# Key/value sums per head: four column-tiled matmuls of 33 columns in one PSUM bank, instead of one matmul of 129 columns over three banks

## The chip, the cores and the metric

One core of one Trainium2 chip. Times are device microseconds (us) of a whole execution, median of the runs named. The profile's span is about 1.7 us shorter than the time of the same execution (723.5 against 725.28 us for the kernel before). All runs here are with a granted TensorE clock of 0.999 to 1.0.

## The reference, cut to what matters

```python
# x: 1 x 2048 x 1024 bf16; 32 heads of 32; F = 3584
q, k, v = heads(layernorm(x) @ wqkv)
phi = lambda t: where(t > 0, t + 1, exp(t)) + 1e-6
kv  = einsum("bhsd,bhse->bhde", phi(k), v)      # 32 x 32 per head, summed over 2048 tokens
z   = einsum("bhsd->bhd", phi(k))
o   = (phi(q) @ kv) / (phi(q) @ z + 1e-6)       # per head
h   = x + o @ wo
out = h + (relu(h' @ W_gate) * (h' @ W_up)) @ W_down     # h' = layernorm(h)
```

The change touches the sums kv and z.

Some terms: a matmul multiplies a stationary operand, which a weight load brings in, by a moving operand. Its output goes to PSUM, here eight banks (0 to 7) of 128 partitions. In a row tile the stationary operand takes only some of the partitions that it is read from, in a column tile only some of the columns, and so the output only some of its partitions. A semaphore is a counter that one engine increments and another waits for.

## The kernel before

Tokens come in 16 tiles of 128. The projections k, v and q are computed in groups of seven products of 4 matmuls (128x128 by 128x512), called P1 to P7, for two token tiles at a time. ScalarE copies partial sums from PSUM bank to PSUM bank within a group, and TensorE adds to the copies. After the v group of a pair of token tiles, TensorE adds that pair to the key/value sums: eight head groups of four heads each, for each of two token tiles, so a block of 16 matmuls. There are eight such blocks.

A matmul multiplies all four heads of phi(k) by all four heads of v and a column of ones. Only the four 32x32 blocks on the diagonal, and the ones column, are wanted.

```python
KVB = [0, 1, 2]                  # three banks hold the sums
P1_POOL = [3, 4, 5, 6, 7]        # banks of the k and v groups

def kv_out(g, w=P + 1):          # GPB = 3 head groups per bank
    c0 = (g % GPB) * KZW
    return ps[:, KVB[g // GPB], c0:c0 + w]

def kvacc(st):                   # st: token tile
    sv = st % NV
    pa = pk_ap(st)               # phi(k) of this tile, 128 tokens x 1024
    for g in range(NG):          # 8 head groups
        ...
        mm(kv_out(g), pa[:, g * P:(g + 1) * P], vv[:, sv, g, 0:P + 1],   # 128x128 by 128x129
           first, st == NST - 1, ...)

def kvfin():                     # ten ScalarE copies pick out the diagonal blocks and the ones column
    ...
        for h in range(HPG + 1):
            ...
            copy(kvz[sl, g0:g0 + n, co]..., src[sl, :, :, cs])
    return steps
...
for h_ in (1, 3, 4, 7):          # spread over q groups two to four
    if kvc:
        hooks[h_] = kvc.pop(0)
```

`hooks[i]` is run after the i-th product of a group. The later attention numerators (`a2_num`) multiply phi(q) by these sums: 32 matmuls of 33 columns per token tile, in four row tiles of 32 partitions.

## Time and profile before

| what | number | where |
|---|---|---|
| time | 725.62 us (725.58 to 725.95, 4 runs) | runs |
| TensorE busy | 717.1 of 723.5 us | page, busy table |
| a block of key/value sums | 0.94 us, eight of them 7.5 us | timeline of TensorE |
| ten copies of the sums on ScalarE | 173 to 324 ns each | the tile's view |
| q groups beside the copies, and others | 6.28, 6.33, 6.51; 6.14 us | timeline of TensorE |

From the page, the busy table and the chain of work that ended last:

```profile
PE 717.1 (99%) x4521; PEld 384.6 (53%) x4521; DVE 587.2 (81%) x1024; ACT 361.0 (50%) x632; POOL 109.5 (15%) x177
PE 89%; DVE 6%; ACT 2%; issue 1%; SPq 1%; DMA 1%; POOL 0%; DVEq 0%; ACTq 0%
```

TensorE is busy nearly always, and the chain runs through it. The waits of TensorE (engine, who it waited for, total us, times, longest):

```profile
PE ps L767 <- POOL RXH L546: 1.4, 1, 1.4
PE ps L767 <- DVE RXH L1252: 0.7, 1, 0.7
PE ps L767 <- ACT ps L772: 0.2, 1, 0.2
```

So little is waited. Now one block in the timeline of TensorE. The columns are start in us, time until the last of the merged instructions ends, engine, line, operation, output and inputs, shape, and how many:

```profile
74.12 1.03 PE L767 MATMUL ps<-RW,RAB 128*128 128x512 f16 x4
74.99 1.10 PE L767 MATMUL ps<-RE 128*128 128x129 bf16 x16
75.93 1.02 PE L767 MATMUL ps<-RAB,RH 128*128 128x512 bf16 x4
76.79 1.03 PE L767 MATMUL ps<-RAB 128*128 128x512 bf16 x4
```

Read starts, not durations: ends are modelled and overlap the next instruction. From 74.99 to 75.93 us is 0.94 us for 16 matmuls, 58.7 ns each. A product of four matmuls of 512 columns takes 0.86 us by the same reading.

The numerators, in the same view (the second column of `32*128` is the stationary operand: 32 rows, 128 columns):

```profile
172.28 0.37 PE L767 MATMUL ps<-kvz,RAB 32*128 32x33 bf16 x32
172.58 3.63 PE L767 MATMUL ps<-RW,RE 128*128 128x512 bf16 x16
```

32 matmuls with 32 weight loads pass in 0.30 us, because four row tiles work at once.

Last, what the copies do. The timeline of ScalarE (ACT) and TensorE inside the fourth q group; PEld is the weight load, and brackets show idle time before and what ended it:

```profile
138.58 0.22 ACT L772 ACTIVATE kvz<-ps 32x64 bf16<-32x64 f32 x1
138.82 0.60 ACT L772 ACTIVATE RXH<-ps 128x512 f32<-128x512 f32 x1
...
139.31 0.59 ACT L772 ACTIVATE ps<-ps 128x512 f32<-128x512 f32 x1
...
139.95 0.55 PEld L767 LDWEIGHTS ps<-RWG,RH 128*128 128x128 f16 x4 [0.59 <-ACT ps L772]
139.96 1.04 PE L767 MATMUL ps<-RWG,RH 128*128 128x512 f16 x4
```

ScalarE does a small copy of the sums (kvz) first, then the two copies that belong to the group. The bank-to-bank copy (ps from ps) ends late, and TensorE starts its product at 139.96 instead of about 139.70, 0.86 us after the product before.

### The profile page before, as it was taken

Reading aid. Unit: us, or ns where it says so; the run is one execution under the profiler, and the core shown is the slowest. Engines: PE = TensorE matmul, PEld = TensorE weight load, DVE = VectorE, ACT = ScalarE, POOL = GpSimd, SP = SyncE. Lnnn points to the kernel's source line nnn. Section 1 sums busy time; section 2 is a strip of 40 time slices with the busy share of each in tenths; the row PEclk is TensorE's granted clock in tenths of the full one; section 3 lists DMA queues with packets and bytes.
Section 4 is the critical chain, followed back from the end, with each engine's and each line's share of the span. In section 5 each row is a group of like instructions: output and inputs, shape, how many; then the busy total and the mean of one; then the engine's idle time right before and its main releaser. Section 6 shows DMA issues by size and latency. Waiting matters only on the chain.

```text
span 723.5 us, 12104 instructions
## 1 busy us (share of the span) xinstructions
PE 717.1 (99%) x4521; PEld 384.6 (53%) x4521; DVE 587.2 (81%) x1024; ACT 361.0 (50%) x632; POOL 109.5 (15%) x177
## 2 busy tenths in 40 slices
PE   9999999999999999999999999999999999999998
PEld 4444444344444444444444568865555555547887
DVE  7878867799776889888988787787889877887984
ACT  4878666764841456687757111035455545423010
POOL 1411100000360103322321002310000000000331
PEclk9999999999999999999999999999999999999999
DMA  9652244023998897999999999994555572037996
GB/s 316 207 115 61 37 131 156 13 29 68 195 229 258 245 267 228 281 296 264 326 298 276 302 265 315 320 211 119 149 166 140 158 248 81 1 102 252 315 321 174
DMA packets 192986, 143.59 MB, mean 198 GB/s; under 512 B 51872, under 2 KB 170400, under 8 KB 192928
## 3 DMA queue, kind: packets, MB, share of 16 engines
q1 hardware_dynamic: 188224, 138.50, 66.6%
q0 software_dynamic: 4032, 3.67, 3.6%
q8 instruction: 35, 0.57, 0.3%
q10 hardware_dynamic: 672, 0.66, 0.3%
q14 instruction: 23, 0.19, 0.1%
HBM read 98.76 MB, written 32.51 MB: 181 GB/s over the span
## 4 chain that ended last, share of the span: by engine, by line
PE 89%; DVE 6%; ACT 2%; issue 1%; SPq 1%; DMA 1%; POOL 0%; DVEq 0%; ACTq 0%
PE ps L767 89%; SPq L565 1%; DVE RAB L853 1%; DMA RE<-in_A_x_dram 1%; DVE RE L1228 1%; DVE RX L850 1%; ACT RX L846 1%; DVE RX L1069 1%; ACT RXH L805 1%; DVE RW L963 0%; DVE RWG L988 0%; ACT ps L772 0%; DVE RE L853 0%; DVE rden L1226 0%; DVE RE L1661 0%
## 5 line engine op out<-in xcount | busy, mean ns | idle before, releaser
L772 ACT ACTIVATE ps<-ps 128x512 f32<-128x512 f32 (+1 forms) x192 | 108.8, 567 | 218.0 <-PE ps L767 210.8
L767 PE MATMUL ps<-RC,RO 128*128 128x512 f16 x616 | 143.0, 369 | 0.0
L767 PE MATMUL ps<-RH,RWG 128*128 128x512 bf16 x448 | 108.1, 379 | 0.0
L767 PEld LDWEIGHTS ps<-RC,RO 128*128 128x128 f16 x616 | 60.3, 98 | 63.5
L767 PE MATMUL ps<-RC,RWG 128*128 128x512 f16 x320 | 76.8, 380 | 0.1
L767 PEld LDWEIGHTS ps<-RH,RWG 128*128 128x128 bf16 x448 | 43.8, 98 | 46.9
L767 PE MATMUL ps<-RH,RO 128*128 128x512 bf16 (+1 forms) x256 | 61.2, 379 | 0.0
L1470 DVE TENSOR_TENSOR RAB<-ps,RAB 128x512 bf16<-128x512 f32 x56 | 37.3, 686 | 29.4 <-PE ps L767 29.3
L767 PE MATMUL ps<-RW,RE 128*128 128x512 bf16 x256 | 57.6, 380 | 0.7 <-DVE RXH L1252 0.7
L1670 POOL DMA_DIRECT2D out_dram<-RX x20 | 17.9, 1256 | 263.3 <-DVE RX L1661 221.0
L767 PE MATMUL ps<-RAB 128*128 128x512 bf16 (+2 forms) x270 | 57.1, 351 | 0.1
L767 PE MATMUL ps<-RW,RAB 128*128 128x256 f16 (+3 forms) x362 | 52.9, 301 | 0.0
L767 PEld LDWEIGHTS ps<-RC,RWG 128*128 128x128 bf16 (+1 forms) x320 | 30.0, 98 | 40.0 <-ACT ps L772 6.0
L772 ACT ACTIVATE RE<-ps 128x512 f32<-128x512 f32 (+1 forms) x64 | 31.5, 503 | 37.8 <-PE ps L767 37.8
L767 PEld LDWEIGHTS ps<-RW,RAB 128*128 128x128 f16 (+1 forms) x362 | 35.4, 98 | 14.4 <-DVE RX L1661 0.2
L1354 DVE TENSOR_TENSOR RO<-RWG 128x1024 f16<-128x1024 bf16 x54 | 37.0, 684 | 6.4 <-DMA RWG<-in_B_W_up_dram 4.7
L1661 DVE TENSOR_TENSOR RE<-ps,RE 128x512 f32<-128x512 f32 x44 | 30.2, 687 | 14.3 <-PE ps L767 13.8
L772 ACT ACTIVATE RAB<-ps 128x512 bf16<-128x512 f32 x56 | 33.3, 594 | 16.6 <-PE ps L767 16.3
L767 PEld LDWEIGHTS ps<-RH,RO 128*128 128x128 f16 (+1 forms) x256 | 24.4, 98 | 30.0 <-ACT RX L772 1.6
L1456 DVE TENSOR_TENSOR RAB<-ps,RE 128x512 bf16<-128x512 f32 x56 | 37.1, 685 | 2.8 <-PE ps L767 1.9
L767 PEld LDWEIGHTS ps<-RW,RE 128*128 128x128 bf16 x256 | 24.0, 98 | 28.7 <-DVE RXH L1252 1.2
L1465 ACT ACTIVATE RAB<-RAB 128x1024 bf16<-128x1024 bf16 x28 | 29.5, 1055 | 19.4 <-DVE RAB L1456 18.9
(163 smaller groups left out, 1168.7 us busy)
## 6 DMA issues: line engine op xcount, KB each, us to landing
RWG<-in_B_W_gate_dram SPq DMA_DIRECT2D x28, 512.0 KB, 6.8
RWG<-in_B_W_up_dram SPq DMA_DIRECT2D x28, 512.0 KB, 5.5
RW<-l_scr SPq DMA_DIRECT2D x20, 448.0 KB, 5.8
RW<-in_B_W_down_dram SPq DMA_DIRECT2D x14, 512.0 KB, 5.7
t_scr<-RW SPq DMA_DIRECT2D x14, 512.0 KB, 5.0
l_scr<-RX SPq DMA_DIRECT2D x7, 1024.0 KB, 5.9
RE<-l_scr SPq DMA_DIRECT2D x15, 448.0 KB, 4.5
RE<-in_A_x_dram SPq DMA_DIRECT2D x23, 256.0 KB, 3.3
```

The costliest lines, as they stand in the source:

```text
L565: return PL.add(eng, lambda e: e.dma_start(dst_ap, src_ap), reads=reads, writes=writes, slot=slot, name=name)
L767: lambda e: e.matmul(out_ap, lhsT, rhs, start=start, stop=stop, skip_group_check=skip),
L772: PL.add("act", lambda e: e.activation(out=dst, in_=src, func=func), reads=reads, writes=writes, name=name)
L805: PL.add("act", lambda e: e.activation(out=junk[:, c0:c1], in_=src[:, c0:c1], func=func, scale=scale, accum_out=sv[:, col:col + 1]), reads ...
L846: PL.add("act", lambda e: e.activation(out=Et[:, k, :], in_=src, func=ACTF.Exp), reads=[src_buf], writes=[B_E[k]], name=name + "_exp")
L850: PL.add("dve", lambda e: e.tensor_scalar(out=Et[:, k, :], in0=Et[:, k, :], scalar1=1.0, scalar2=1e-6, op0=ALU.min, op1=ALU.add), reads=[] ...
L1354: PL.add(eng, lambda e: e.tensor_tensor(out=tb(j, u), in0=f0(u), in1=f1(u), op=ALU.subtract), reads=[B_w[i + x] for x in r] + ([B_T[k + x] ...
L1456: PL.add("dve", lambda e: e.tensor_tensor(out=d, in0=src, in1=ftmp[:, u, :], op=ALU.add), reads=[bsrc, B_s5[u]], writes=[db], name=name)
L1465: PL.add("act", lambda e: e.activation(out=d, in_=d, func=ACTF.Relu), reads=[], writes=db, name=name)
L1470: PL.add("dve", lambda e: e.tensor_tensor(out=d, in0=bank(b), in1=d, op=ALU.mult), reads=[B_bank[b]], writes=[db], name=name)
L1661: PL.add(eng, lambda e: e.tensor_tensor(out=dst, in0=in0, in1=in1, op=op), reads=reads, writes=writes, name=name)
L1670: PL.add("pool", lambda e: e.dma_start(dst, src, accum_op=ALU.add), reads=[bsrc], writes=[B_hscr[st]], slot=sl, name="acc_%d_%d" % (st, dh))
```

## The change

Its intent: compute only the diagonal blocks. Each head's 32 columns of phi(k) become one column tile of TensorE, with output in that head's 32 partitions, and the moving operand is that head's 32 columns of v and a column of ones. That needs v stored in runs of 33 instead of 130 columns per head group. The sums fit one bank, one copy evacuates them, and two banks go to the k and v groups.

```diff
+    HW = Dh + 1                      # 33
+    VW = HPG * HW
@@
-        KVB = [0, 1, 2]
-        P1_POOL = [3, 4, 5, 6, 7]
+        KVB = 0
+        P1_POOL = [1, 2, 3, 4, 5, 6, 7]
@@ def kvacc(st):
-                mm(kv_out(g), pa[:, g * P:(g + 1) * P], vv[:, sv, g, 0:P + 1],
-                   first, st == NST - 1, [B_pk[pk_slot(st)][half], B_v[sv][half], B_vones], B_bank[kb],
-                   "kvacc_%d_%d" % (st, g), skip=True)
+                for h in range(HPG):
+                    c0 = g * P + h * Dh
+                    mm(ps[h * Dh:(h + 1) * Dh, KVB, g * HW:(g + 1) * HW], pa[:, c0:c0 + Dh],
+                       vh[:, (st % NV) * H + g * HPG + h, :], False, st == NST - 1,
+                       [B_pk[pk_slot(st)][half], B_v[st % NV][half], B_vones], B_bank[KVB],
+                       "kvacc_%d_%d" % (st, g), skip=True)
@@ def kvfin():           (the ten copies, cut)
+            touch_bank(KVB)
+            ident_act(kvz[:, :, 0:HW], ps[:, KVB, 0:NG * HW].rearrange("p (g w) -> p g w", w=HW), [B_bank[KVB]],
+                      [B_kvz], "kvc")
@@
-        pe_dummies(12, P1_POOL)
+        pe_dummies(12, P1_POOL + [KVB])      # also zeroes the bank of the sums
@@
-                if r == 0 and ct == 1:
-                    kvc = kvfin()
-                if r == 0 and ct >= 1:
-                    for h_ in (1, 3, 4, 7):
-                        if kvc:
-                            hooks[h_] = kvc.pop(0)
+                if r == 0 and ct == 1:
+                    hooks[1] = kvfin
```

The v copies and the column of ones are adapted to the new layout (cut).

More of the change, by code (lines that the diff above doesn't have):

```diff
@@ L171, in bass_sequential_preLN__linear_attn_block__glu_gated_reglu__prompt_kernel @@
     NKV = 2 * ND2
-    VW = P + 2
-    KZW = P + HPG
-    GPB = 3
+    HW = Dh + 1
+    VW = HPG * HW
     GPN = NW // P
@@ L265, in bass_sequential_preLN__linear_attn_block__glu_gated_reglu__prompt_kernel @@
         o0 += NPK * D
-        vv = RE[:, o0:o0 + NV * NG * VW].rearrange("p (a g w) -> p a g w", a=NV, g=NG)
+        vh = RE[:, o0:o0 + NV * NG * VW].rearrange("p (n w) -> p n w", w=HW)
         def pk_slot(st):
@@ L412, in bass_sequential_preLN__linear_attn_block__glu_gated_reglu__prompt_kernel @@
         B_E = bufs("E_", NPH)
-        B_kvz = bufs("kvz_", 2 * (HPG + 1))
+        B_kvz = _Buf("kvz")
         B_pqT = [[bufs("pqT%d_%d_" % (r, t), NG) for t in range(2)] for r in range(2)]
@@ L555, in bass_sequential_preLN__linear_attn_block__glu_gated_reglu__prompt_kernel @@
         )
-        PL.add("pool", lambda e: e.memset(vv[:, :, :, P:VW], 1.0), writes=[B_vones], name="vones")
+        PL.add("pool", lambda e: e.memset(vh[:, :, Dh:HW], 1.0), writes=[B_vones], name="vones")
         PL.add("pool", lambda e: e.memset(neghalf[:], -0.5), writes=[B_neghalf], name="neghalf")
@@ L860, in phi @@
                 f_()
-        KVB = [0, 1, 2]
-        P1_POOL = [3, 4, 5, 6, 7]
-        def kv_out(g, w=P + 1):
-            c0 = (g % GPB) * KZW
-            return ps[:, KVB[g // GPB], c0:c0 + w]
+        KVB = 0
+        P1_POOL = [1, 2, 3, 4, 5, 6, 7]
         def run(ops, n):
@@ L945, in v_out @@
         def v_out(st, j):
-            return vv[:, st % NV, j * GPN:(j + 1) * GPN, 0:P]
+            n0 = (st % NV) * H + j * GPN * HPG
+            return vh[:, n0:n0 + GPN * HPG, 0:Dh]
         def gw(ap):
-            return ap.rearrange("p (g w) -> p g w", w=P)
+            return ap.rearrange("p (n w) -> p n w", w=Dh)
         def v_copy(b, st, j):
@@ L1164, in q_group @@
                    add_phi(*dst(1, 1), "q_%d_%d" % (r, ct)), "q%d%d" % (r, ct), hooks)
-        kv_started = [False] * 8
         def kvacc(st):
-            sv = st % NV
             pa = pk_ap(st)
@@ L1172, in kvacc @@
                 half = (g * P) // NW
-                kb = KVB[g // GPB]
-                first = not kv_started[kb]
-                kv_started[kb] = True
-                mm(kv_out(g), pa[:, g * P:(g + 1) * P], vv[:, sv, g, 0:P + 1],
-                   first, st == NST - 1, [B_pk[pk_slot(st)][half], B_v[sv][half], B_vones], B_bank[kb],
-                   "kvacc_%d_%d" % (st, g), skip=True)
-        def kvfin():
-            for b_ in KVB:
-                touch_bank(b_)
-            rb = [B_bank[b_] for b_ in KVB]
-            steps = []
-            def copy(out, in_):
-                b_ = B_kvz[len(steps)]
-                steps.append(lambda: ident_act(out, in_, rb, [b_], "kvc"))
-            for b0, nb, ng, g0 in ((0, 2, GPB, 0), (2, 1, NG - 2 * GPB, 2 * GPB)):
-                src = ps[:, b0:b0 + nb, 0:ng * KZW].rearrange("p b (g w) -> p b g w", w=KZW)
-                n = nb * ng
-                for h in range(HPG + 1):
-                    sl = slice(h * Dh, (h + 1) * Dh) if h < HPG else slice(0, P)
-                    cs = sl if h < HPG else slice(P, P + 1)
-                    co = slice(0, Dh) if h < HPG else slice(Dh, Dh + 1)
-                    copy(kvz[sl, g0:g0 + n, co].rearrange("p (b g) w -> p b g w", b=nb), src[sl, :, :, cs])
-            return steps
-        A_POOL = [[3, 4, 5, 6, 7], [4, 5, 6, 7]]
+                for h in range(HPG):
[4 more added lines that the diff above has]
+                       "kvacc_%d_%d" % (st, g), skip=True)
+        def kvfin():
+            touch_bank(KVB)
+            ident_act(kvz[:, :, 0:HW], ps[:, KVB, 0:NG * HW].rearrange("p (g w) -> p g w", w=HW), [B_bank[KVB]],
+                      [B_kvz], "kvc")
+        A_POOL = [P1_POOL[2:], [4, 5, 6, 7]]
         NB = [0, 1, 2, 3]
@@ L1213, in a2_num @@
                     mm(ps[:, NB[h], g * NUW:g * NUW + Dh + 1], pqT[sl, r, t, g, i * P:(i + 1) * P],
-                       kvz[sl, g, 0:Dh + 1], True, True, [B_pqT[r][t][g]] + B_kvz, B_bank[NB[h]],
+                       kvz[sl, g, 0:Dh + 1], True, True, [B_pqT[r][t][g], B_kvz], B_bank[NB[h]],
                        "num_%d_%d" % (st, g), skip=True)
```

## The prediction

> What bounds the kernel now. TensorE. The page's busy table gives PE 717.1 of 723.5 us (99%), the chain that ended last is 89% PE, and the view of waits shows 2.3 us of PE waits, 0.2 us of them between 20 and 170 us. A microsecond of TensorE stream removed there should come off the end.
>
> Where the change works. The timeline of TensorE shows eight blocks of sixteen 128x129 matmuls (two token tiles times eight head groups) between 35 and 124 us. From the start of a block to the start of the next matmul is 0.94 us (35.24 to 36.18, 48.67 to 49.61), 58.7 ns per matmul. All eight: 7.5 us, 1.0% of the span. That is nearly the whole prize.
>
> After: each block is 64 weight loads of 32 columns and 64 matmuls of 33, in sixteen sets of four column tiles. The kernel has a similar stream already: the attention numerators, 32 matmuls of 33 columns in four row tiles. In the trace's single start times each set of four takes 25 ns there (172.316, .341, .366, .391), and from the last start to the next ordinary matmul is 0.10 us. The Trainium skill, "TensorEngine Tiling (Array Packing)", Key Properties, says that different tiles can load weights and multiply in parallel and that changing the tiling mode drains TensorE; the trace agrees for row tiles (25 ns for four; about 0.1 us on leaving). The same page, Restrictions and Gotchas, says that column tiling excludes Fast Weight Load; no trace here has a column tile, so this is my largest doubt.
> My estimate for a block, if column tiles run like row tiles: 16 x 25 ns = 0.40, plus 0.10 to leave, up to 0.1 to enter and for waits in the stream: 0.60 us. Saved: 0.34 x 8 = 2.7 us.
>
> The copies of the sums on ScalarE: ten (173 to 324 ns, by the tile's view) become one of 128x264, estimated 0.38 us from the shapes measured (32x64 210 ns, 32x192 318 ns). Between 123 and 143 us they delay the bank-to-bank copies that TensorE waits for: the q groups without them take 6.14 us, the three with them 6.28, 6.33 and 6.51, 0.70 us lost. The one copy costs about 0.1 of that again. Saved: 0.6 us.
>
> Moved, expected to cost nothing: the values are written in runs of 32 instead of 128 (VectorE's similar op with runs of 32 takes 1225 ns per 1024 elements, against 690 per 512); two PSUM banks are freed, but TensorE hardly waits for a bank; 384 more weight-load and matmul pairs are fetched and dispatched.
>
> Sum: 725.6 - 2.7 - 0.6 = 722.3; with some weight on slower column tiles I say 722.8 us, 80% range 721.2 to 727.0. Faster by over 2%: 1%; within 2%: 96%; slower by over 2%: 3%.
>
> What would show it: in the timeline the eight blocks as 64 matmuls of 128x33, about 0.6 us to the next matmul, 25 ns per set of four; all q groups near 6.14 us; VectorE and ScalarE times per instruction unchanged; everything after 148 us about 3 us earlier.
>
> What would make it wrong: weight loads of column tiles going one after another (at 25 ns each a block takes about 1.7 us: 731 in all); dispatch of 128 instructions not keeping up; 66-byte steps that misalign the odd heads and slow the moving reads or value writes; the earlier work turned into waits for the weight DMAs after 169 us (DMA engines are 93 to 98% busy from 169 to 460 us).

## The result, and the profile after

723.75 us (723.53 to 723.92, 4 runs) against 725.62: 1.87 us less. The ratio of the fast runs is 0.9973, 95% interval 0.9956 to 0.999. A ratio here is the mean time of one kernel's fast runs over that of the other's of the same rounds, so not quite the ratio of the medians. The result of the kernel is correct.

The page's lines:

```profile
PE 714.2 (99%) x4905; PEld 380.4 (53%) x4905; DVE 587.5 (81%) x1024; ACT 359.2 (50%) x623; POOL 108.4 (15%) x177
PE 90%; DVE 6%; issue 1%; ACT 1%; POOL 1%; DMA 0%; ACTq 0%; DVEq 0%
```

384 more matmuls, 9 fewer ScalarE instructions, the same bound. The waits of TensorE (line numbers are shifted by the change):

```profile
PE ps L766 <- POOL RXH L545: 1.4, 1, 1.4
PE ps L905 <- DVE RXH L834: 1.1, 1, 1.1
PE ps L766 <- DVE RXH L1229: 0.7, 1, 0.7
PE ps L766 <- ACT ps L771: 0.5, 1, 0.5
PE ps L766 <- DVE RWG L984: 0.4, 1, 0.4
```

Three waits are new or longer: 1.1, 0.5 and 0.4 us. All lie before 40 us. The same block as above:

```profile
74.22 1.03 PE L766 MATMUL ps<-RW,RAB 128*128 128x512 f16 x4
75.18 0.70 PE L766 MATMUL ps<-RE 128*32 128x33 bf16 x64
75.81 1.04 PE L766 MATMUL ps<-RAB,RH 128*128 128x512 bf16 x4
76.69 1.03 PE L766 MATMUL ps<-RAB 128*128 128x512 bf16 x4
```

Two things are to be seen. The block itself takes 75.18 to 75.81, 0.64 us. And the product ahead of it lasts 74.22 to 75.18, 0.96 us instead of 0.86: entering the column-tiled stream costs 0.09 us. So a block costs 0.73 us, not 0.94. All eight blocks are alike to 2 ns.

Why 0.64? These are the times from one set of four matmuls to the next in this block, in ns, from the start times of single matmuls (the last figure includes 110 ns from the last matmul to the next ordinary one):

```
set       1   2   3   4   5   6   7   8 |  9  10  11  12  13  14  15   16
after    38  25  25  26  25  27  25  26 | 33  37  33  56  36  34  33  159
```

The first eight sets go at 25 ns, like the row tiles of the numerators. From the ninth on a set takes 33 to 37 ns, and two sets have about 22 ns more; the matmul that comes late is each time one that increments a semaphore.

The copies of the sums, in the tile's view, are one (min, median and max ns; first and last start), where before it had ten:

```profile
L771 ACT ACTIVATE kvz<-ps x1: 387/387/387, 124.8 to 124.8; 128x264 bf16<-128x264 f32 x1
```

Q groups two to four now take 6.20, 6.15 and 6.13 us. The value writes in runs of 32 cost nothing: medians of 687 to 694 ns on VectorE and 595 ns on ScalarE, against 684 to 691 and 592.

To see where a gain or a loss arises, I compare starts of the same VectorE instruction, whose order is the same in all kernels here. The lead is how much earlier it starts than in the profile of before:

| at (us in before) | 12.9 | 46.6 | 61.3 | 89.8 | 107.5 | 122.3 | 142.3 | 189 | 338 | 720 |
|---|---|---|---|---|---|---|---|---|---|---|
| lead of after | -0.32 | -0.32 | -0.18 | +0.04 | +0.41 | +0.57 | +1.41 | +1.43 | +1.43 | +1.44 |

It starts 0.32 us behind, because the first load of x ended later in this execution (VectorE's first instruction starts at 3.59 us, in before at 3.27). Until 46.6 us the lag stays 0.32 to the hundredth: the first block's saving does not show. From there the lead grows, and what is gained by 142 us stays to the end.

### The profile page after: what moved, and what is told of

The parts are those of the page before. It is cut to its first block, busy times and chain, and to the rows that moved or that the text cites. A ratio compares the mean times of both kernels' runs of the same rounds, so it can differ in the third digit from the quotient of the medians.

```text
span 722.1 us, 12877 instructions
## 1 busy us (share of the span) xinstructions
PE 714.2 (99%) x4905; PEld 380.4 (53%) x4905; DVE 587.5 (81%) x1024; ACT 359.2 (50%) x623; POOL 108.4 (15%) x177
## 4 chain that ended last, share of the span: by engine, by line
PE 90%; DVE 6%; issue 1%; ACT 1%; POOL 1%; DMA 0%; ACTq 0%; DVEq 0%
PE ps L766 90%; DVE RAB L852 1%; DVE RE L1205 1%; DVE st L780 1%; DVE RX L849 1%; POOL rstd L790 0%; DVE RW L959 0%; DMA RE<-in_A_x_dram 0%; DVE RC L959 0%; DVE RX L1065 0%; ACT RX L845 0%; ACT RXH L804 0%; DVE RXH L834 0%; DVE rden L1203 0%; ACT ps L771 0%
## 5 line engine op out<-in xcount | busy, mean ns | idle before, releaser
L766 PEld LDWEIGHTS ps<-RAB 128*128 128x128 bf16 (+1 forms) x270 | 26.0, 98 | 24.4 <-ACT RAB L908 1.0
```

Of the source, the lines that this page charges most:

```text
L766: lambda e: e.matmul(out_ap, lhsT, rhs, start=start, stop=stop, skip_group_check=skip),
```

## The experiments

Theory. (1) A block costs 0.73 us because the first 64 instructions (32 pairs of weight load and matmul) stand ready when it starts, and from then on the issue of instructions limits: about 8.3 ns per pair, more for one that increments a semaphore. (2) The first block's saving is lost since VectorE sets the pace up to about 40 us. (3) The copies gave back what they cost. Rivals are named with each run. All were timed in five rounds, in three series; the time of before in them was 725.99, 725.75 and 725.92 us. Each has one profile. In the profiles of most of these runs the record of the first matmul after six of the eight blocks is missing (4849 of 4905 matmuls recorded), so where I give a block's time I take it from the two that have it.

### rep_after: the changed kernel again

> The changed kernel again, unaltered: 723.75 +- 0.3 us. It gives a second profile, to see how much of the start varies by itself: the first load of x ended 0.32 us later in the profile of after than in that of before, and VectorE stayed exactly 0.32 us late until 42 us. If that is chance of the load, the offset is another one here (0.0 to 0.4 us); if the change causes it, it is 0.32 again. The blocks must again take 0.64 us from their first matmul to the next ordinary one.

723.95 us (723.79, 723.80, 723.95, 724.05, 725.00). Blocks 0.638 us. VectorE's first instruction starts at 3.49 us, in the other twelve profiles of changed kernels between 3.33 and 3.59. So it varies from execution to execution; the profile of before, at 3.27, had the earliest of all. The start is not the whole lag, though: in nine of the thirteen VectorE loses another 0.04 to 0.28 us at about 27 us. In the profile of rep2_after (below) the lag goes from 0.06 to 0.32 us there: ScalarE waits 1.00 us for a load of x at 21.44 us, TensorE then waits for ScalarE, and at 28.20 us VectorE does. Whether this second part is chance or comes with the change, the one profile of before does not tell. One execution in five was 1 us slower, but its span, 722.0 us, is that of the others: what it lost lies outside the span, so it is not the late transposes of below.

### g_outer: another order of the same 64 pairs

```diff
         def kvaccs(p):
-            kvacc(2 * p)
-            kvacc(2 * p + 1)
+            for g in range(NG):
+                kvacc(2 * p, [g])
+                kvacc(2 * p + 1, [g])
```

> In each block the head group is the outer loop and the token tile the inner one (same 64 pairs, another order). Theory (the first 64 instructions stand ready when the block starts, from then on issue limits): pairs 1 to about 33 again at 25 ns per set of four, the rest at about 33 ns, block 0.64 us, time 723.7 +- 0.3. Rival A (adding to columns that the set just before also added to is slow): every second set slow from the start. Rival B (the second token tile's addresses are slow): every second set slow from the start, the block as long as now.

723.95 us (one execution of 725.01, again with a span of 722.0); blocks 0.639 us. The sets of a block:

```
set       1   2   3   4   5   6   7   8 |  9  10  11  12  13  14  15   16
g_outer  40  25  25  25  25  25  25  29 | 33  37  33  34  33  33  56  161
```

The change of pace is at the same place although other data stand there: rivals A and B fall. The longer set has moved from 12 to 15, to where this order has its increments; the increments that fall within the first eight sets cost nothing.

### split: two bursts of 32 pairs

```diff
                 def v6(p=p, nq=nq):
-                    kvaccs(p)
+                    kvacc(2 * p)
...
-                v_group(p + 2, {2: v2, 3: v3, 5: v5, 6: v6})
+                v_group(p + 2, {2: v2, 3: v3, 5: v5, 6: v6, 7: lambda p=p: kvacc(2 * p + 1)})
```

(and likewise for the last two blocks)

> The two token tiles of a block are put one product of 4 matmuls apart, so two bursts of 32 pairs. Theory (queue of 64 instructions, then issue-bound): all sets of both bursts at 25 ns; each burst 0.09 to enter + 0.21 + 0.10 to leave = 0.40, two 0.80 instead of 0.73 us, so 0.5 us slower than after in all (724.2). Rivals (the second token tile is slow for its addresses or for adding to written columns): second burst at 33 ns per set, 0.90 us for both, 1.2 us slower (724.9).

724.47 us, 0.52 more than rep_after beside it. The timeline of TensorE:

```profile
75.47 0.38 PE L766 MATMUL ps<-RE 128*32 128x33 bf16 x32
76.01 0.81 PE L766 MATMUL ps<-RAB,RH 128*128 128x512 bf16 x3 [0.16 <-issue]
76.75 0.38 PE L766 MATMUL ps<-RE 128*32 128x33 bf16 x32
77.06 0.60 PE L766 MATMUL ps<-RAB 128*128 128x512 bf16 x2
```

(In the second line the first of four matmuls is not recorded, hence "x3" and a wait that was none.) Both bursts run all their sets at 25 ns, the second token tile too. A burst takes 0.31 us and 0.09 to enter, two 0.81 us instead of 0.73. The theory's number was 0.80. This run settles the main point of (1): the slow half is a matter of how many pairs follow one another, not of which. That it is the issue of instructions that limits there is inferred from the count of 64 and the even pace; no record shows it. It shows as well that the fast pace alone does not pay, as each burst pays for entering and leaving.

### one_inc: one increment per block instead of four

The last matmul of a block is noted as the reader of everything that the block read, so the earlier ones need not increment.

```diff
+        def last_reads(st):
+            return [b for s_ in ([st - 1, st] if st % 2 else []) for b in B_pk[pk_slot(s_)] + B_v[s_ % NV]]
...
-                       [B_pk[pk_slot(st)][half], B_v[st % NV][half], B_vones], B_bank[KVB],
+                       [...] + (last_reads(st) if g == NG - 1 and h == HPG - 1 else []), B_bank[KVB],
```

> A block's readers are noted at its last matmul, so that one matmul of 64 increments the semaphore instead of four. Theory (in the issue-bound half an increment costs about 22 ns more of issue): the pause of 31 ns in the middle of the second half goes, the block takes 0.61 instead of 0.64 us, 0.2 us faster in all (723.5). Rival (the pauses come from the waits or the place in the stream): the pause stays, time as after.

723.48 us, 0.47 less than rep_after. Blocks 0.597 us; sets 9 to 15 all take 31 to 38 ns, and the 56 is gone. The lead at 142 us is 1.75 instead of 1.42 us. The pause came from the increment.

### two_tiles: two column tiles of 64

```diff
-                for h in range(HPG):
+                for h in range(0, HPG, 2):
...
-                    mm(ps[h * Dh:(h + 1) * Dh, KVB, g * HW:(g + 1) * HW], pa[:, c0:c0 + Dh],
-                       vh[:, (st % NV) * H + g * HPG + h, :], ...
+                    mm(ps[h * Dh:(h + 2) * Dh, KVB[g // 4], (g % 4) * 2 * HW:(g % 4 + 1) * 2 * HW], pa[:, c0:c0 + 2 * Dh],
+                       vh[:, n0:n0 + 2, :], ...
```

(KVB is [0, 1], six banks for the groups, four copies of 32x264 at products 1 and 3 of the second q group and 1 of the next two)

> Two column tiles of 64 instead of four of 32: 32 pairs a block, 66 moving columns, output in two banks, four copies of 32x264. Theory (the first 64 instructions stand ready, a set lasts as long as its columns stream: 66 columns about 30 ns): 16 sets of 30 ns, block 0.59 us from first matmul to the next ordinary one instead of 0.64, 0.3 us gained in the blocks, 0.2 to 0.3 us lost to the copies: time as after within 0.3 us. Rival (a weight load of 64 columns[...] is slower than the stream): sets of 50 ns or more, block 0.9 us, 1.5 us slower than after.

724.56 us. The sets of two take 29 to 36 ns, 32 on average, the block 0.63 us. By the products' pace (216 ns for 512 columns) I estimate 28 ns for 66 columns, so this is near the pace of the stream; the rival (50 ns or more) falls, and weight loads of 64 columns are nearly hidden. But the gain over 0.64 is little, and the copies cost far more than I expected: between 122 and 142 us its lead goes from 1.12 to 1.06 us, where that of after grows by 0.84. The expected time was missed by 0.3 us for the copies.

### ten_copies: the old copies in the changed kernel

```diff
+            for g0, n in ((0, 6), (6, 2)):
+                for h in range(HPG):
+                    copy(slice(h * Dh, (h + 1) * Dh), g0, n, 0, Dh)
+                copy(slice(0, P), g0, n, Dh, HW)
...
+                    for h_ in (1, 3, 4, 7):      # as before
```

> The changed kernel, but the sums are copied out in ten pieces of the shapes of before, at the same places in the q groups. Theory: q groups two to four take 6.28, 6.33 and 6.5 us again instead of 6.15, the kernel is 0.6 to 0.7 us slower than after (724.6). Rival (the q groups got faster by the freed banks or by an earlier VectorE): no more than 0.2 us slower.

724.70 us. No run of after stood in this series (ten_copies, skip1, skip4 and five_banks); in the other two it took 723.95 and 723.92. The lead at 142 us is 0.81 instead of 1.41 us: the copies are worth 0.60 us (0.66, if the lead is counted from 46.6 us on), nearly all of the 0.70 us that the q groups lost before. (3) holds.

### skip1 and skip4: one block left out

Their outputs are wrong, which doesn't matter for the times.

```diff
         def kvaccs(p):
+            if p == 0:          # skip4: p == 3
+                return
             kvacc(2 * p)
```

> Wrong result on purpose: the changed kernel without the first block of the key/value sums (0.73 us of TensorE at 35 us). Theory (up to about 40 us VectorE, which starts with the first load of x and never idles, decides when TensorE may go on): TensorE waits the 0.73 us away at the first product after it that needs VectorE or ScalarE, time within 0.15 us of after. Rival (TensorE binds throughout): 0.73 us faster.

> Wrong result on purpose: the changed kernel without the fourth block (0.73 us of TensorE at 75 us). Theory (TensorE binds from about 47 us on): 0.55 to 0.73 us faster than after, a little lost to gaps as TensorE moves ahead of ScalarE and VectorE. Rival (VectorE binds there as well): under 0.3 us faster.

By the time both missed: 724.72 and 724.54 us, each slower than after in the other two series. The profile takes this apart:

| lead (us) at | 46.6 | 142.3 | 189 | 338 | 720 |
|---|---|---|---|---|---|
| after | -0.32 | 1.41 | 1.43 | 1.43 | 1.44 |
| skip1 | -0.32 | 1.39 | 1.41 | 0.03 | 0.05 |
| skip4 | -0.19 | 2.21 | 2.24 | 0.68 | 0.68 |
| five_banks (below) | -0.30 | 1.70 | 1.72 | 0.81 | 0.82 |

Up to 189 us both theories hold. Without the whole first block, 0.73 us of TensorE, skip1 leads as after does: that block is off the critical path. Without the fourth, skip4 leads by 0.80 us more (0.67, counted from 46.6 us on). One product of TensorE starts at 39.39 us with the first block and without it, in after and then in skip1 (which had also waited 0.22 us more at 33.88 us, just before the place of the block):

```profile
39.39 1.04 PE L766 MATMUL ps<-RC,RWG 128*128 128x512 f16 x4 [0.53 <-ACT ps L771]
```

```profile
39.39 1.04 PE L766 MATMUL ps<-RC,RWG 128*128 128x512 f16 x4 [0.96 <-ACT ps L771]
```

That the first block is off the critical path, as (2) has it, is shown. That VectorE sets the pace there is so only in part: ScalarE is busy without a pause before this product, since a wait for VectorE that ended at 36.95 us; but VectorE does idle before that (0.5 to 1.0 us at 12, 20 and 22 us), and in nine profiles it loses time at about 27 us, as said above. But then, between 189 and 338 us, skip1 loses 1.4 and skip4 1.6 us. The waits in the timeline of TensorE, skip1 and then skip4:

```profile
199.68 3.61 PE L766 MATMUL ps<-RW,RE 128*128 128x512 bf16 x16 [0.62 <-DMA RE<-RE]
...
219.36 10.52 PE L766 MATMUL ps<-RW,RE 128*128 128x512 bf16 x47 [0.62 <-DMA RE<-RE]
```

```profile
199.14 3.61 PE L766 MATMUL ps<-RW,RE 128*128 128x512 bf16 x16 [0.92 <-DVE rden L1203]
```

These are the output matmuls of the attention, which need a DMA transpose of the attention output (RE from RE). The profile names VectorE in skip4, whose instruction ended at 199.12, just before TensorE started at 199.14. But the transpose that was issued at 192.33 us landed at 199.01, and the trace has the instruction (L118) with which TensorE waits for this transpose's semaphore: it ran at 199.04. In skip1 the transpose landed at 199.54, this instruction ran at 199.57 and TensorE started at 199.68; in five_banks 199.01, 199.04 and 199.14. So it was the transpose each time. In after it landed at 198.39 for matmuls that could start at 198.97. So it has 0.58 us to spare there, and a TensorE that comes earlier, or a transpose that is slower, uses that up. The second waits, at 219.36 in skip1 and at 222.17 us in skip4, are of the same kind, for transposes issued at 214.11 and 216.22 us.

### five_banks: the freed banks lie idle

```diff
-        P1_POOL = [1, 2, 3, 4, 5, 6, 7]
+        P1_POOL = [3, 4, 5, 6, 7]
```

> The changed kernel, but the k and v groups keep the five PSUM banks of before (3 to 7); two banks lie idle. Theory (the freed banks are worth nothing, and the small new gaps of TensorE in the k and v groups come from ScalarE and VectorE being later than TensorE): time as after, 723.9 +- 0.3 in this series. Rival (the other rotation of seven banks makes the gaps): the eleven to fifteen gaps go, a k+v pair takes 12.95 instead of 13.02 us, 0.3 to 0.4 us faster. Third (the two freed banks help TensorE): slower by 0.3 us or more.

724.40, 724.31, 724.28, 723.35, 723.32 us: two kinds of executions, 0.9 us apart. The profile is of the slower kind, and its waits are the late transposes again. Up to 189 us it leads by 1.72 instead of 1.43 us, and the pair of a k and a v group with its block takes 12.96 instead of 13.02 us. Small gaps before products, of 33 to 50 ns, are four in most pairs of after and three in five_banks as in before: two come and one goes. So my theory that the freed banks are worth nothing falls, in the direction of the rival: a rotation over all seven costs 0.3 us. How the rotation over seven banks makes the two gaps (one ahead of P3 of the k group, one ahead of P5 of the v group) I did not find out. It is not that any use of the freed banks costs: two_tiles rotates over six, has two such gaps, and its pair without the block takes 12.28 us, against 12.32 over five and 12.38 over seven. This is most of why it leads by 1.12 us at 122 us, where after leads by 0.57. Six banks with four column tiles were not run.

### Last series: rep2_after, inc_five, inc_five_early

inc_five is one_inc and five_banks together. inc_five_early also moves two weight loads of the next stage:

```diff
-            if t in (5, 7, 18, 19):
+            for _ in range({4: 2, 18: 1, 19: 1}.get(t, 0)):
                 load_w_next()
```

> The changed kernel once more, as the measure for the three beside it on the same chip. At 142 us 1.4 us ahead of before, as in its two profiles. If the waits of 0.4 to 0.9 us for the transposes of the attention output (199 to 222 us) that fell on five_banks, skip1 and skip4 are chance of an execution or of a chip, they fall on some executions here too (724.7 to 725.2 instead of 723.8); if they belong to those kernels, on none or one in five.

> The changed kernel with one increment per block and the five banks of before: both gains add, block 0.60 us, a k+v pair 12.93 us, 2.0 us ahead of before at 142 us. Time 723.1 in executions without waits in the attention output, about 1 us more in those with; rival (the gains share a cause): no more than 1.75 us ahead at 142 us.

> As inc_five, but the two loads of gate weights of 512 KB that the queue issued at about 183 and 193 us, just ahead of transposes of the attention output, are issued at about 176 us, when the DMA engines are half idle. Theory (these loads make the transposes land too late for the output matmuls): TensorE waits for no transpose and nothing that hangs on one between 190 and 225 us, all five executions within 0.4 us, 723.1. Rival (the waits come from other transfers, or from the order of the queue): waits and spread as in inc_five.

| kernel | five executions (us) | median | lead at 142 | at 720 |
|---|---|---|---|---|
| rep2_after | 724.15 723.84 724.41 723.92 723.92 | 723.92 | 1.38 | 1.06 |
| inc_five | 723.29 723.88 724.15 724.14 723.38 | 723.88 | 1.93 | 1.94 |
| inc_five_early | 723.20 723.18 723.32 723.30 723.26 | 723.26 | 2.03 | 2.06 |

rep2_after has the late transposes in its profile too (it loses 0.33 us about 205 us), so they are not a matter of the altered kernels alone. inc_five leads by 1.93 us, so both gains add, but three of its five executions are 0.5 to 0.9 us slower than its best. (Its profile is of a fast execution and shows no such wait.) The DMA queue of skip4 and of inc_five_early (SPq is the issuing engine, the second column how long issuing took):

```profile
191.63 0.58 SPq L564 DMA_DIRECT2D RWG<-in_B_W_gate_dram  x1
192.33 2.46 SPq L568 DMA_TRANSPOSE RE<-RE  x1
```

```profile
175.94 1.18 SPq L564 DMA_DIRECT2D RWG<-in_B_W_gate_dram  x2
...
191.68 1.24 SPq L568 DMA_TRANSPOSE RE<-RE  x1
```

Right behind a weight load of 512 KB, issuing the transpose took 2.46 us and it landed 6.68 us after its start. This is the extreme: the transpose behind that load takes 4.5 to 5.7 us in the other profiles that have the load there, but for skip1's 6.65 (4.60 in after). With the loads moved to 176 us it took 1.24 and 3.15 us: it landed at 194.83, 3.5 us ahead of need. No wait for a transpose is left between 190 and 225 us, and the five executions lie within 0.14 us. So moving the loads does away with the late executions: none of five here, three of five in inc_five. The first waits of skip1 and skip4, at 199 us, are for the transpose behind the load. Their second waits are not: there the queue holds loads of x (256 KB) and stores, no weight load, and I did not find out why they were late. Nor do the runs tell whether a load holds the transpose up in the queue or by taking the DMA engines. At 723.26 us (ratio to before 0.9963, interval 0.9951 to 0.9976) it is the fastest kernel here, 0.66 us below the changed one beside it, and correct.

What stays open: how often an execution meets the late transposes. All five of skip1 and of skip4 were slow for their lead. Of the fourteen executions of after two, both in rep2_after, have a longer span (722.4 against 721.8 to 722.3 us). Whether that is the chip (they ran on another than rep_after) or the kernel, no run tells.

## Why the prediction was right

The range (721.2 to 727.0) and the class held; the measured 723.75 us is 0.95 above the point and 1.4 above the sum of 722.3. The range is so wide that it takes in the time of before, so that the number alone says little; what was tested is the mechanism. It was right, and the terms of the sum were off as follows.

| term | predicted saving (us) | measured (us) | shown by |
|---|---|---|---|
| eight blocks | 8 x 0.34 = 2.7 | 8 x 0.209 = 1.67 | profile of after; split, one_inc |
| of these, the first block | counted in | -0.21: off the critical path | skip1 |
| copies of the sums | 0.6 | 0.60 | ten_copies |
| two freed banks | 0 | -0.28 | five_banks |
| sum | 3.3 | 1.78 | times: 1.87 |

The two profiles differ by 1.44 us at the end, or 1.76 counted from 46.6 us on; the 0.32 us between is the lag of the start, which the table leaves out.

- "TensorE. [...] A microsecond of TensorE stream removed there should come off the end." Right from about 47 us on. Wrong for the first of eight blocks: I had read the whole window from the share of busy time, and did not ask who sets the pace in the first 40 us. A busy TensorE was no proof.
- "if column tiles run like row tiles: 16 x 25 ns = 0.40". Right for the first eight sets. The step that was mis-sized is this term: the second eight take 33 to 37 ns and the increments come on top. A burst of 32 pairs was the longest that the profile of before had, and I drew its pace out to 64. I named "dispatch of 128 instructions not keeping up" as a risk, and what came fits it, in a mild form.
- "plus 0.10 to leave, up to 0.1 to enter and for waits": 0.11 and 0.09. Together with the stream (0.53 instead of 0.40 us) a block costs 0.73 instead of 0.60.
- "column tiling excludes Fast Weight Load [...] my largest doubt". The Trainium skill ("TensorEngine Tiling (Array Packing)", Restrictions and Gotchas) says so; in these traces no cost of it shows: sets of four loads of 32 columns keep 25 ns, sets of two loads of 64 columns 32 ns on average.
- The copies: 0.6 predicted, 0.60 measured; one copy of 387 ns, 380 predicted.
- "VectorE and ScalarE times per instruction unchanged": right, within 3 ns.
- "two PSUM banks are freed, but TensorE hardly waits for a bank": it gained nothing, and the rotation over all seven lost 0.28 us.
- "the earlier work turned into waits for the weight DMAs after 169 us": not in the profile of after, whose lead stays 1.43 from 189 us on. The danger was real, though, with a different transfer: transposes, the first of them delayed behind weight loads. (In the profile of before the DMA engines are busy for 97% of 169 to 460 us on average, but only for 51% of 170 to 182 us, which is where inc_five_early put its loads.) It took 0.33 us of one profile of the changed kernel, and more of the faster variants.

## What to carry to other kernels

A stream of small tiled matmuls runs at its best pace only while the instructions queued ahead last; when you double the longest burst that you have measured, measure again, and let few of its matmuls increment a semaphore. A saving counts only where its engine sets the pace, so look stage by stage at which engine's timing is fixed; leaving a piece of work out, wrong result and all, tells it in one run, if the profile is read and not only the time. When a faster variant comes out slower, line the same instruction up in both traces: here the gain was there until 189 us and was given back to a transfer with half a microsecond to spare.

## What the Trainium skill lacked or had wrong

- "TensorEngine Tiling (Array Packing)", Key Properties: switching the tiling mode drains TensorE, without a number. Here 0.09 us on entering and 0.11 us (0.12 in one_inc, 0.13 in two_tiles) from the last small matmul to the next ordinary one, for bursts of 32 and of 64 pairs.
- "TensorE: Matmul & The Clock Gate", Part 1 (the section on 56 ns): it says that start-to-start never drops below about 25 ns however small N is. Here this holds for each tile: a set of four in different tiles, each with its own weight load, takes 25 ns. The section does not say that the floor counts per tile; over the four it is 6.3 ns per pair, and 8.3 ns in the issue-bound half.
- The same page, the table of specifications, gives TensorE a queue of 64 instructions. The traces agree: the pace changes after 32 to 33 pairs, in two orders of the pairs, and never in bursts of 32. What the pace is once the queue is used up no page says: 33 to 37 ns per set of four.
- The same page, Part 3, "The cost: per-tile semaphore tail": 26.3 ns per increment. Here about 22 ns in the issue-bound half, and nothing in the half that stands ready.
- The same page, Part 3, "What overlaps and what doesn't": weight loads overlap matmuls in flight only when the row group differs. Here column tiles share all row groups, and their loads were still hidden (25 ns per set); the plain products, too, start a matmul every 216 ns with weight loads of 98 ns. That bullet is narrower than the Part's own paragraph on the mechanism, which also lets a load go ahead into the background weight buffer.
- No page has that a DMA transpose right behind a 512 KB load in the same queue lands late: 4.6 us after its issue in after and 6.7 us in skip4, instead of 3.2 without the load. Some transposes further from a load take long as well (5.9 us for the one issued at 188.29 us in after).
